# Preparing the second pass's weights later, and taking chunk one last: one core of Trainium2

## The chip, the cores and the metric

The kernel runs on one core of a Trainium2 chip. The metric is the device time of one execution in microseconds (us), as the median of several. The core has TensorE (PE; its weight loads are listed apart as PEld), VectorE (DVE), ScalarE (ACT), GpSimd (POOL), and SyncE (SP), which here issues the DMAs.

## The reference

```python
scores = scale * np.matmul(q, k.transpose(0, 1, 3, 2))        # 8 batches, 8 heads, 576 x 64
...
mask = (rel >= 0) & (rel < window)                            # window 128
scores = np.where(mask, scores + bias[None], -1000000000.0)   # bias: -slope * |i - j|
...
attn_out = np.matmul(attn, v)                                 # softmax of scores, times v
x = attn_out.transpose(0, 2, 1, 3).reshape(B * S, H * D)      # 4608 x 512
h = x @ w_in                                                  # 512 x 2048
sp = np.maximum(h, 0.0) + np.log1p(np.exp(-np.abs(h)))
g = h * erf(sp)
out = g @ w_out                                               # 2048 x 512
```

## The kernel before

**Attention.** It runs in 48 steps, one for the same pair of heads in all that a load `qk` brings; the names carry the step's number: `qk44`, the scores of step 44 on PE (line 635), the masked rows `p44` and sums `st44` on DVE (669), exponentials on ACT (677), scaling on POOL (700), a transpose on DVE (717, `pa44`) and the product with v on PE (739). Four steps make one chunk of 384 tokens of x. There are 12 chunks. All but the first few go through DRAM (`xd`, written at line 791, read as `xr` at 942 or, in the second pass, as `y` at 1113).

**The feed-forward part, first pass** (`one_pass`). Every matrix product is made of three TensorE products of fp32r values: high part by high part, high by low, low by high. The hidden axis of 2048 is cut into 16 tiles of 128 (in the names: `wti`, `wto` 0 to 15 for a tile of w_in or w_out). The first pass takes tiles 0 to 5 of each chunk, 72 units in all, with their weights resident in the tile `w1`; it is interleaved with attention. A unit is a product with w_in (line 977), a copy of its 128x384 sum out of a PSUM bank into `hs` (959 on ACT or 963 on DVE; this pass has one such bank), and later a product with w_out (1053). In between, the activation of several units is made together (a flush, `activate`): softplus and erf on ACT with three table loads (1020, 1022, 1024), a multiplication on DVE (1032), a cast `gh` and a remainder `gl` (1036). After a chunk's six units its output sums go to DRAM as `pd0` to `pd35`, one for 128 tokens (1071).

**Second pass** (`blocks_pass`). The other ten tiles are taken as five pairs, p = 0 to 4, for six double chunks C of 768 tokens: 30 rounds R. A round multiplies a 2x2 block of w_in by a 2x2 block of x in seven products instead of eight (`pair`, products at 1158, their sums combined at 1164 to 1169), activates, and multiplies with w_out (1196: 36 matmuls, three for each of two hidden tiles and six token tiles). Each round fetches its weights from DRAM (`fetch`, 1102: `wi`, 1792 KB, and `wo`, 1024 KB). In a double chunk's last round `store` (1062) loads the first pass's sums (`ot<-pd`, 1073), adds PE's sums on DVE (1074) and stores the result (1079). There are `OB` = 3 buffers `ot`.

**Pair weights.** What `fetch` reads is prepared once by `Weights.pair` (865). For each pair two tiles of w_in and two of w_out are decoded (`decode`, 806: a raw load `wri` or `wro`, one step on ACT or POOL at 823/825, one on ACT at 831, three on DVE at 834, 836, 838), four sums are made for the seven products (876 to 879, `ws`), and each of the parts wa, wb, wc, wd (w_in) and we (twice, w_out) is split into high and low (`split`, 853: a cast at 959 to 963, a subtract at 859) and stored to DRAM (861). The fetch of `wi4` waits for the stores of all four parts of pair 4. The first raw load of each pair waits for the load of one head-pair step, number `WN + p * WD`.

**What sets the order.** Nothing is ordered by hand. `Plan.run` (284) simulates all engines at build time and writes each engine's instructions in the order in which it places them. Each operation has an `at`. Among an engine's ready operations whose buffers are free the smallest `at` goes first:

```python
if o.ready > t + self.WAIT[e] + 1e-9 or (best and (best.at, best.seq) < (o.at, o.seq)):
    continue
if fits(o) and all(t + o.costs[e] <= max(free[x], t) + c for x, c in o.costs.items()):
    best = o
```

So `at` is a priority, not a time; on the chip every engine takes its instructions strictly in the order written, and waits at each for its semaphores. `LEAD` and `TM` make the `at` of the first pass (unit U at LEAD + U * TM, and t1 = LEAD + 72 * TM is the start of the second), `TR` that of its rounds, `W2A` and `W2B` that of the pair weights.

Of the kernel before, what the change touches and what calls it, by code (L numbers as in the profile page):

```python
# [8 lines left out]
F32 = mybir.dt.float32  # L9
# [10 lines left out]
P = 128  # L20
WIN = 128
DM = H * D
# [25 lines left out]
TE, NE = 2.0, 28  # L48
TA = 1.8
LL, LP, LT = 18, 6, 0  # L50
TM = 4.3
LEAD = 70
TR = 15.5
XL, XS = 60, 30
MC, MP, MH = 0.01, 16, -20
W1A, W1B, W1C = 20, 5, 0.4
W2A, W2B, WL = 150, 30.0, 36
WN, WD = 18, 1
POOLQ, POOLH, POOLX, POOLG = 0, 0, 0, 0


# [137 lines left out]
class View(Buf):  # L199
# [10 lines left out]

    def __getitem__(self, at):
        return self.all[at]


class Banks:
# [675 lines left out]
class Moe:  # L891
# [170 lines left out]
    def store(self, u, t, po, at):  # L1062
        nc, op = self.nc, self.plan.op
        T = u["c"] * (self.width // P) + t
        ot = Buf(self.op_, [P, DM], F32, "o", OB, f"ot{T}_{u['U']}")
        part = self.part[T]
        nbytes = P * DM * 4
        if self.first:
            op({"DVE": dve(DM), "Act": act(DM, src=0.06)},
               lambda e: self.copy(e, ot.all, po.all), r=[po], w=[ot], at=at)  # L1070
            op(emit=lambda e: nc.sync.dma_start(part.ap, ot.all), r=[ot], w=[part], at=at, **dma(nbytes))
        else:
            op(emit=lambda e: nc.sync.dma_start(ot.all, part.ap), r=[part], w=[ot], at=at - 10, **dma(nbytes))
            op({"DVE": dve(DM)}, lambda e: nc.vector.tensor_tensor(  # L1074
                ot.all, po.all, ot.all, ALU.add), r=[po, ot], w=[ot], at=at)

            def rows(e):
                for o, r0, n in rows_of(T):
                    nc.sync.dma_start(self.out[r0 : r0 + n, :], ot[o : o + n])  # L1079

            op(emit=rows, r=[ot], at=at, **dma(nbytes, len(rows_of(T))))

    def blocks_pass(self, wi, wo, pool, home, gone, time):

        nc, op = self.nc, self.plan.op
        self.first, self.width = False, 2 * CH
        tags = ["o0", "o1", "o2", "h", "a0", "a1"]
        R = 0
        for C in range(self.nt // (2 * CH)):
            x = self.load_blocks(C, time(R), pool, home, gone)  # L1090
            po = [Buf(self.ps, [P, DM], F32, tag, 1, f"q{C}_{tag}") for tag in tags]
            for p in range(NP):
                own, over = home["wi"] if R % 3 == 2 else (Buf(pool, [P, 14 * SB], F32, "wi", 2, f"wi{R}"), [])
                a = self.fetch(wi[p], own, over * (R == 2), 14 * SB, gone, time(R) - WL)
                own = Buf(pool, [P, 4 * DM], F32, "wo", 3, f"wo{R}")
                b = self.fetch(wo[p], own, [], 4 * DM, gone, time(R) - WL + 0.6 * TR)
                self.pair(C, p, R, x, a, b, po, time(R))
                R += 1
# [3 lines left out]
        op(emit=lambda e: nc.sync.dma_start(w.all, src[0].whole.ap), r=[*src, gone], w=[w, *over], at=at, **dma(P * n * 4))  # L1102
        return w

    def load_blocks(self, C, at, pool, home, gone):

        nc, op = self.nc, self.plan.op
        begun = C == 0
        raw = [Buf(self.xp if t == 0 else pool, [P, NK, CH], F32, "xr", 1, f"y{C}_{t}") for t in range(2)]
        half = lambda b, k: Part(b, slice(None), slice(2 * k, 2 * k + 2))  # L1110
        b = [[half(y, k) for k in range(2)] for y in raw]
        for t in range(2):
            op(emit=lambda e, t=t: nc.sync.dma_start(raw[t].all, self.x_dram[2 * C + t].ap),
               r=[gone, *self.x_parts[2 * C + t]], w=b[t], at=at - XL, **dma(P * NK * CH * 4))
        whole = Buf(pool, [P, 6, CH], F32, "xt", 1, f"xt{C}")
        t1, t2, t4 = (Part(whole, slice(None), slice(2 * k, 2 * k + 2)) for k in range(3))

        def minus(out, a, c):
            op({"DVE": dve(2 * CH)}, lambda e: nc.vector.tensor_tensor(out.all, a.all, c.all, SUB),
               r=[a, c], w=[out], at=at - XS)  # L1120

        minus(t1, b[1][0], b[0][0])
        minus(t2, b[1][1], t1)
        minus(t4, b[0][1], t2)
        minus(b[1][0], b[1][1], b[1][0])
        x = {}
        for n, (name, src) in enumerate([
                ("B11", b[0][0]), ("B21", b[0][1]), ("T2", t2), ("T1", t1), ("T3", b[1][0]), ("B22", b[1][1]), ("T4", t4)]):
            over = []
            if name in home:  # L1130
                hi, lo, over = home[name]
            else:
                hi = Buf(self.xp, [P, 2, CH], F32R, "xh", XB, f"yh{C}_{n}")
                lo = Buf(self.xp, [P, 2, CH], F32R, "xl", XB, f"yl{C}_{n}")
            over = over * begun
            op({"DVE": dve(2 * CH, True), "Act": act(2 * CH), "Pool": pool_cast(2 * CH)},
               lambda e, hi=hi, src=src: self.copy(e, hi.all, src.all), r=[src], w=[hi, *over], at=at - XS + 0.01 * n)
            op({"DVE": dve(2 * CH)}, lambda e, hi=hi, lo=lo, src=src: nc.vector.tensor_tensor(
                   lo.all, src.all, hi.all, SUB), r=[src, hi], w=[lo, *over], at=at - XS + 0.01 * n)
            x[name] = hi, lo  # L1140
        return x

    def pair(self, C, p, R, x, wi, wo, po, at):

        nc, op = self.nc, self.plan.op
        first, last = p == 0, p == NP - 1
        hs = [Buf(self.hp, [P, MW], F32, "m", MB, f"hs{R}_{j}", keep=KH) for j in range(2)]
        h = [[Part(y, slice(None), slice(CH * t, CH * t + CH)) for t in range(2)] for y in hs]

        def product(ps, a, c, begin):  # L1150
            xh, xl = x[c]
            ah, al = LEFT[a]

            def emit(e):
                for k in range(2):
                    w = lambda o: wi[:, o + P * k : o + P * k + P].bitcast(F32R)
                    for n, (o, y) in enumerate(((ah, xh), (ah, xl), (al, xh))):
                        nc.tensor.matmul(  # L1158
                            ps[:, :CH], lhsT=w(o), rhs=y[:, k], start=(begin and k + n == 0), stop=(k + n == 3),
                            skip_group_check=not begin)  # L1160

            op({"PE": 6 * f32r_us(CH) + 0.015}, emit, r=[wi, xh, xl] + [ps] * (not begin), w=[ps], at=at + MH)

        def read(ps, to):
            op({"Act": act(CH, src=0.06), "DVE": dve(CH)}, lambda e: self.copy(e, to.all, ps[:, :CH]),
               r=[ps], w=[to], at=at + MH)

        def add(ps, to):
            op({"DVE": dve(CH)}, lambda e: nc.vector.tensor_tensor(to.all, ps[:, :CH], to.all, ADD),  # L1169
               r=[ps, to], w=[to], at=at + MH)  # L1170

        z, v, u = (Buf(self.ps, [P, 512], F32, "z", 2, f"{k}{R}") for k in "zvu")
        product(z, "A11", "B11", True)
        read(z, h[0][0])
        product(v, "A12", "B21", True)
        add(v, h[0][0])
        product(z, "S2", "T2", False)
        read(z, h[0][1])
        product(u, "S1", "T1", True)
        product(z, "S3", "T3", False)  # L1180
        read(z, h[1][1])
        add(u, h[1][1])
        product(u, "S4", "B22", False)
        add(u, h[0][1])
        product(z, "A22", "T4", False)
        read(z, h[1][0])
        g = self.activate([(MW, hs[j], h[j], at + MC, f"{R}_{j}") for j in range(2)])
        for j in range(2):
            gh, gl = g[j]
            for t in range(2 * CH // P):  # L1190

                def mm(e, j=j, t=t, gh=gh, gl=gl):
                    cs = slice(P * t, P * t + P)
                    w = [wo[:, DM * (2 * j + k) : DM * (2 * j + k + 1)].bitcast(F32R) for k in range(2)]
                    for n, (gg, k) in enumerate(((gh, 0), (gh, 1), (gl, 0))):
                        nc.tensor.matmul(  # L1196
                            po[t].all, lhsT=gg[:, cs], rhs=w[k],
                            start=(first and j + n == 0), stop=(last and j + n == 3),
                        )

                op({"PE": 3 * f32r_us(DM) + 0.015}, mm, r=[gh, gl, wo], w=[po[t]], at=at + MP)
                if last and j:
                    self.store(dict(c=C, U=R), t, po[t], at + MP)


@with_exitstack
def tile_kernel(ctx, tc, qk, vb, w_in, w_out, plain, bias, out, nb=B):
# [63 lines left out]
    wo = [pieces(b, 0, 1024, 2048) for b in drams[1]]  # L1271
    for p in range(NP):
        w1.later = [attention.loaded[min(WN + p * WD, len(attention.loaded) - 1)]]
        w1.pair(p, NF1 + 2 * p, wi[p], wo[p], W2A + p * W2B)
    home, c0 = {}, 0
    for name, n, k in (("wi", 14 * SB, 1), ("T1", 2 * CH, 2), ("T3", 2 * CH, 2), ("B22", 2 * CH, 2), ("T4", 2 * CH, 2)):
        if name == "T3":
# [81 lines left out]
```

## Time and profile before

| | us |
|---|---|
| median of 3 runs | 987.21 (986.49 to 991.13) |
| the profiled execution, device time | 984.83 |
| its span in the trace | 983.0 |
| PE busy | 938.8 (95% of the span) |
| DVE busy | 629.5 (64%) |
| ACT busy | 638.5 (65%) |
| POOL busy | 169.6 (17%) |

The span is the time from the first to the last recorded work; the device time is 1.8 us longer. Times of the trace count from the start of the span. The stages on the time axis: attention with the first pass to about 400 us, the rest of the first pass and the first rounds of the second mixed to about 560, then only rounds of the second pass to the end. PEclk is the granted TensorE clock, 1.00 at 2.4 GHz.

### The profile page before, as it was taken

The page shows a single profiled execution, that of the slowest core. Times are in us where ns is not written, and L with a number is a line of the kernel's source. Part 1 is how long each engine was busy: PE and PEld are TensorE (multiplying, and loading weights), DVE is VectorE, ACT ScalarE, POOL GpSimd, SP SyncE. Part 2 cuts the span into 40 slices and gives each one's busy share as a digit, 9 for nine tenths or more (in the row PEclk, how much of TensorE's full clock was granted, in tenths as well). Part 3 has the DMA queues.
Part 4 walks back from the last instruction along what each step waited for, and adds up shares of the span by engine and source line. Part 5 has one row for each costly group of instructions (what it writes and reads, how often), then busy time and mean ns, then how long its engine had stood idle before and what let it go on. Part 6 is the DMA issues. An engine that isn't in the chain of part 4 may idle for free.

```text
span 983.0 us, 26558 instructions
## 1 busy us (share of the span) xinstructions
PE 938.8 (95%) x11080; PEld 815.2 (83%) x11080; DVE 629.5 (64%) x1468; ACT 638.5 (65%) x1290; POOL 169.6 (17%) x304
## 2 busy tenths in 40 slices
PE   8868999999999999999999999999999999999995
PEld 7656878778877787899988898998988899898984
DVE  6888688888888898444565564564464385373432
ACT  7877777777786688565736746656565666566460
POOL 3544244425445443200000000000000000000000
PEclk9998999999999999999999999999999999999998
DMA  7774667788877776471445658566676756855613
GB/s 242 244 235 148 189 212 232 249 267 283 296 271 259 256 229 228 170 279 58 150 176 210 220 197 328 192 260 224 259 261 220 274 208 225 279 213 177 230 43 97
DMA packets 58760, 216.06 MB, mean 220 GB/s; under 512 B 6928, under 2 KB 16144, under 8 KB 50960
## 3 DMA queue, kind: packets, MB, share of 16 engines
q1 hardware_dynamic: 58640, 214.36, 62.8%
q8 instruction: 87, 1.43, 0.6%
q14 instruction: 33, 0.27, 0.1%
HBM read 171.61 MB, written 42.73 MB: 218 GB/s over the span
## 4 chain that ended last, share of the span: by engine, by line
PE 63%; DMA 2%; DVE 1%; POOL 1%; issue 0%; SPq 0%; ACT 0%; DVEq 0%; POOLq 0%
PE banks L1196 24%; PE banks L1158 21%; PE banks L1053 8%; PE banks L977 7%; PE banks L739 2%; DMA ot<-pd 2%; PE banks L635 1%; DMA out_dram<-ot 1%; POOL p L700 1%; DVE ot L1074 0%; DVE p L669 0%; SPq L1079 0%; DVE pa L717 0%; DVE hs L963 0%; SPq L1102 0%
## 5 line engine op out<-in xcount | busy, mean ns | idle before, releaser
L1196 PE MATMUL banks<-wo,gh 128*128 128x512 f32 x720 | 223.6, 391 | 1.3 <-DVE ot L1074 1.3
L959 ACT COPY hs<-banks 128x384 f32<-128x384 f32 x150 | 71.9, 479 | 199.0 <-PE banks L1158 158.4
L700 POOL TENSOR_SCALAR p<-p,st 128x160 f32<-128x160 f32 (+2 forms) x282 | 158.3, 579 | 226.8 <-DVE st L692 148.4
L977 PE MATMUL banks<-xh,w 128*128 128x384 f32 x576 | 170.3, 351 | 8.8 <-ACT hs L959 6.1
L1196 PEld LDWEIGHTS banks<-wo,gh 128*128 128x128 f32 x720 | 133.1, 188 | 22.6 <-DVE ot L1074 2.4
L1053 PE MATMUL banks<-w,gh 128*128 128x512 f32 x432 | 139.9, 405 | 3.1 <-DVE gh L963 1.7
L1196 PE MATMUL banks<-wo,gl 128*128 128x512 f32 x360 | 141.6, 393 | 0.0
L677 ACT ACTIVATE p<-p,st 128x160 f32<-128x160 f32 (+2 forms) x288 | 120.3, 422 | 25.1 <-DVE st L669 23.7
L977 PEld LDWEIGHTS banks<-xh,w 128*128 128x128 f32 x576 | 108.2, 192 | 19.3 <-ACT hs L959 7.6
L1032 DVE TENSOR_TENSOR hs<-s,hs 128x768 f32<-128x768 f32 (+1 forms) x103 | 89.5, 899 | 30.0 <-ACT s L1022 30.0
L1169 DVE TENSOR_TENSOR hs<-banks,hs 128x384 f32<-128x384 f32 x90 | 50.0, 556 | 85.7 <-PE banks L1158 51.1
L977 PE MATMUL banks<-xl,w 128*128 128x384 f32 x288 | 98.5, 342 | 0.5 <-issue 0.5
L1158 PE MATMUL banks<-w,wi 128*128 128x384 f32 x480 | 94.7, 336 | 0.7 <-DVE hs L963 0.7
L1036 DVE TENSOR_TENSOR gl<-hs,gh 128x768 fp32r<-128x768 f32 (+1 forms) x103 | 91.3, 910 | 5.4 <-ACT gh L959 4.2
L1053 PEld LDWEIGHTS banks<-w,gh 128*128 128x128 f32 x432 | 77.3, 189 | 20.1 <-issue 6.3
L1158 PEld LDWEIGHTS banks<-w,wi 128*128 128x128 f32 x480 | 85.1, 188 | 5.7 <-DVE hs L963 1.0
L1053 PE MATMUL banks<-w,gl 128*128 128x512 f32 x216 | 86.0, 398 | 0.1
L1020 ACT ACTIVATE s<-hs 128x768 f32<-128x768 f32 (+1 forms) x103 | 76.2, 793 | 7.2 <-DVE hs L1169 6.8
L1196 PEld LDWEIGHTS banks<-wo,gl 128*128 128x128 f32 x360 | 67.5, 187 | 14.3
L669 DVE CUSTOM_DVE_ANT_0 p<-banks,tables 128x160 f32<-128x160 f32 (+2 forms) x288 | 75.0, 317 | 4.7 <-PE banks L635 4.3
L1022 ACT ACTIVATE s<-s 128x768 f32<-128x768 f32 (+1 forms) x103 | 76.2, 794 | 0.5
L739 PEld LDWEIGHTS banks<-pa,v 32*64 32x64 f32 x4576 | 60.2, 132 | 19.4 <-DVE st L669 9.3
(114 smaller groups left out, 1419.7 us busy)
## 6 DMA issues: line engine op xcount, KB each, us to landing
wi<-wi SPq DMA_DIRECT2D x20, 1792.0 KB, 7.2
wo<-wo SPq DMA_DIRECT2D x30, 1024.0 KB, 7.0
w<-wi SPq DMA_DIRECT2D x10, 1792.0 KB, 7.4
v<-v_b SPq DMA_DIRECT2D x24, 512.0 KB, 4.9
qk<-qk SPq DMA_DIRECT2D x24, 400.0 KB, 5.2
pd<-ot SPq DMA_DIRECT2D x36, 256.0 KB, 4.0
y<-xd SPq DMA_DIRECT2D x12, 768.0 KB, 4.4
ot<-pd SPq DMA_DIRECT2D x36, 256.0 KB, 6.0
```

The source lines that it names most:

```text
L669: nc.vector.tensor_tensor_reduce(out=dst(j), in0=cut(ps[j].all), in1=cut(table[:, half * j + c0 : half * j + c0 + n]), scale=-0.125, scala ...
L677: nc.scalar.activation(dst(j), dst(j), AF.Exp, bias=low[:, j : j + 1], scale=-1.0, accum_out=total[:, j : j + 1])
L700: (nc.vector if e == "DVE" else nc.gpsimd).tensor_scalar(dst, dst, totals[t][:, j : j + 1], 1.0, op0=ALU.mult, op1=ALU.mult)
L739: nc.tensor.matmul(whole[64 * j : 64 * j + 64, first + a, 32 * t0 : 32 * (t0 + n)], lhsT=y.v[rows, 128 * slot + 64 * j : 128 * slot + 64 * ...
L977: nc.tensor.matmul(ps[:, :W], lhsT=ww[:, cs], rhs=xx[:, k], start=(k2 + k + n == 0), stop=(k2 + k + n == 4),)
L1020: A.activation(s[:, :n], hs[:, :n], AF.Softplus)
L1022: A.activation(s[:, :n], s[:, :n], AF.Erf)
L1032: op({"DVE": dve(n)}, lambda e, s=s, hs=hs, n=n: V.tensor_tensor(hs[:, :n], s[:, :n], hs[:, :n], ALU.mult), r=[s, *own], w=[hs], at=at)
L1036: op({"DVE": dve(n)}, lambda e, gh=gh, gl=gl, hs=hs, n=n: V.tensor_tensor(gl[:, :n], hs[:, :n], gh[:, :n], SUB), r=[hs, gh], w=[gl], at=at)
L1053: nc.tensor.matmul(po.all, lhsT=gg[:, cs], rhs=w.all, start=(u["start"] and n == 0), stop=(u["end"] and n == 2),)
L1158: nc.tensor.matmul(ps[:, :CH], lhsT=w(o), rhs=y[:, k], start=(begin and k + n == 0), stop=(k + n == 3), skip_group_check=not begin)
L1196: nc.tensor.matmul(po[t].all, lhsT=gg[:, cs], rhs=w[k], start=(first and j + n == 0), stop=(last and j + n == 3),)
```

## The change

Three things are edited. First, numbers: `LEAD` and `TM` are lowered, so the first pass's priorities come earlier; the raw loads of all pair weights wait for head-pair step 44 (`WN`, `WD`) instead of 18 to 22; and the pair weights' priority is tied to the round that uses them. Second, the second pass takes double chunks 1 to 5 first and 0 last, and the one-off overlays (`begun`) go by round 0 instead of C = 0. Third, the last round, now that of C = 0, gets four more buffers for the sums `ot`: slices (`Strip`) of one tile `ots` in a pool that is otherwise used for x; and in that round the w_out products go tile by tile instead of hidden tile by hidden tile. The stores of chunk 0's rows are one DMA of 128x512 per token tile; other chunks' are partly cut in two or three. Lines of the changed file are 10 to 12 higher up to the store and some 16 to 21 higher behind it.

```diff
-TM = 4.3
-LEAD = 70
+TM = 4.1
+LEAD = 60
...
-W2A, W2B, WL = 150, 30.0, 36
-WN, WD = 18, 1
+W2A, W2B, WL = 40, 8.0, 36
+WN, WD = 44, 0
...
+class Strip(Part):
...
+    @property
+    def all(self):
+        return self.whole.all.rearrange("p a n -> p (a n)")[:, self.c0 : self.c0 + self.n]
...
-        ot = Buf(self.op_, [P, DM], F32, "o", OB, f"ot{T}_{u['U']}")
+        spare = u.get("spare")
+        if spare and t < len(spare):
+            ot = spare[t]
+        else:
+            ot = Buf(self.op_, [P, DM], F32, "o", OB, f"ot{T}_{u['U']}")
...
-        for C in range(self.nt // (2 * CH)):
-            x = self.load_blocks(C, time(R), pool, home, gone)
+        n = self.nt // (2 * CH)
+        for C in [*range(1, n), 0]:
+            x = self.load_blocks(C, R == 0, time(R), pool, home, gone)
...
+        spare = []
+        if last and not C:
+            own = Buf(self.pool, [P, 6, CH], F32, "xt", 1, "ots")
+            spare = [Strip(own, k * DM, DM) for k in range(4)]
...
-        for j in range(2):
+        tiles = range(2 * CH // P)
+        for j, t in [(j, t) for t in tiles for j in range(2)] if last and not C else [(j, t) for j in range(2) for t in tiles]:
...
-                    self.store(dict(c=C, U=R), t, po[t], at + MP)
+                    self.store(dict(c=C, U=R, spare=spare), t, po[t], at + MP)
...
-        w1.pair(p, NF1 + 2 * p, wi[p], wo[p], W2A + p * W2B)
+        w1.pair(p, NF1 + 2 * p, wi[p], wo[p], t1 + p * TR - W2A)
```

What the order becomes, at three places.

ACT ahead of its first table load (the start of the first flush), before; `wqo` and `wuo` are the two decoding steps on ACT, p10 the exponentials of step 10, hs the sums of a unit:

```order
L823 ACTIVATE wqo2_1210<-wro2_1149 128x512
L831 ACTIVATE wuo2_1212<-wro2_1149 128x512
L959 CAST w1_551<-wto1_1180 128x512
L677 ACTIVATE p10_1227,st10_1228<-p10_1227,st10_1228 128x160 x6
L823 ACTIVATE wqo3_1307<-wro3_1178 128x512
L535 COPY xr2_1171<-banks_134 128x384
L831 ACTIVATE wuo3_1339<-wro3_1178 128x512
L959 COPY hs4_2_1345<-banks_134 128x384
L1020 ACT_TABLE_LOAD
L1020 ACTIVATE s0_1353<-hs0_0_758 128x768
```

and now:

```order
L971 COPY hs2_1_1058<-banks_134 128x384
L689 ACTIVATE p9_1070,st9_1071<-p9_1070,st9_1071 128x160 x2
L843 ACTIVATE wuo1_1164<-wro1_946 128x512
L547 COPY xr2_1179<-banks_134 128x384
L835 ACTIVATE wqo1_1182<-wro1_946 128x512
L971 COPY hs4_2_1212<-banks_134 128x384
L1032 ACT_TABLE_LOAD
L1032 ACTIVATE s0_1219<-hs0_0_758 128x768
```

The decoding of w_out tiles 2 and 3, some casts of `w1` and the exponentials of step 10 now stand behind the flush.

ACT and SP in the last of the pair weights, those of pair 4. Now, on ACT (hs3: sums of round 3; its last copy is that of the round's last product) and then on SP:

```order
L971 COPY hs3_1_8355<-banks_134 128x384
L971 CAST gh2_1_8362<-hs2_1_8220 128x768
L971 COPY hs3_1_8355<-banks_134 128x384
L971 CAST wd4_8387<-wti15_8264 128x256
L1032 ACT_TABLE_LOAD
```

```order
L1119 DMA wo3_8279<-wo3_164 128x2048
L873 DMA wi4_160<-wa4_8257 128x1024
L873 DMA wi4_160<-wb4_8308 128x1024
L873 DMA wi4_160<-wc4_8377 128x1024
L873 DMA wi4_160<-wd4_8387 128x2x256
L1119 DMA wi4_8427<-wi4_160 128x3584
L1119 DMA wi6_8433<-wi1_157 128x3584
```

Before, SP stored the same part in the middle of the attention loads (`v44`, `v45`):

```order
L861 DMA wi4_160<-wb4_6383 128x1024
L861 DMA wi4_160<-wc4_6546 128x1024
L529 DMA v45_6802<-v_b 128x896
L861 DMA wi4_160<-wd4_6799 128x2x256
L791 DMA xd10_78<-xs43_6808 128x384
```

The fetch that stood some 40 SP instructions behind the last store now stands right behind it.

SP at the end, before, where three loads stand behind six stores:

```order
L1079 DMA out_0_dram<-ot31_29_11263 64x512
L1079 DMA out_0_dram<-ot31_29_11263 32x512 x2
L1079 DMA out_0_dram<-ot32_29_11271 32x512 x2
L1079 DMA out_0_dram<-ot32_29_11271 64x512
L1073 DMA ot33_29_11576<-pd33_113 128x512
L1073 DMA ot34_29_11578<-pd34_114 128x512
L1073 DMA ot35_29_11580<-pd35_115 128x512
L1079 DMA out_0_dram<-ot33_29_11576 128x512
L1079 DMA out_0_dram<-ot34_29_11578 64x512 x2
L1079 DMA out_0_dram<-ot35_29_11580 128x512
```

and now, where the four loads into `ots` stand some 20 instructions further ahead:

```order
L1089 DMA ot4_29_11263<-pd4_84 128x512
L1089 DMA ot5_29_11271<-pd5_85 128x512
L1119 DMA wo28_11282<-wo3_164 128x2048
L1119 DMA wo29_11387<-wo4_165 128x2048
L1095 DMA out_0_dram<-ots_10921 128x512 x4
L1095 DMA out_0_dram<-ot4_29_11263 128x512
L1095 DMA out_0_dram<-ot5_29_11271 128x512
```

No load stands behind a store of the last chunk any more.

## Rows read from the trace of the kernel before

**Rows 1.** The page, part 1: busy us (share of the span) and instructions of each engine.

```profile
PE 938.8 (95%) x11080; PEld 815.2 (83%) x11080; DVE 629.5 (64%) x1468; ACT 638.5 (65%) x1290; POOL 169.6 (17%) x304
```

**Rows 2.** Stage table; stretch, length, busy us (instructions) by engine, PEclk, DMA share, GB/s.

```profile
25.00:50.00 25.00, 21.07 (x369) 16.27 (x366) 22.28 (x83) 22.18 (x73) 13.99 (x24) 0.93 0.73 247
50.00:75.00 25.00, 17.59 (x447) 14.65 (x440) 21.23 (x62) 19.49 (x55) 10.69 (x18) 0.88 0.76 236
75.00:100.00 25.00, 20.92 (x484) 17.02 (x484) 21.79 (x62) 17.86 (x53) 9.28 (x15) 0.84 0.42 130
100.00:125.00 25.00, 25.00 (x463) 20.81 (x463) 15.57 (x56) 18.66 (x52) 8.34 (x17) 0.94 0.60 185
200.00:300.00 100.00, 95.94 (x2190) 79.46 (x2175) 85.51 (x256) 77.02 (x206) 44.57 (x77) 1.00 0.79 268
400.00:560.00 160.00, 159.00 (x971) 142.93 (x961) 84.17 (x116) 95.28 (x127) 1.38 (x3) 1.00 0.49 180
```

**Rows 3.** Waits of PE, 25 to 100 us: us in total, times, longest.

```profile
PE banks L977 <- ACT hs L959: 6.1, 3, 3.2
```

**Rows 4.** Waits of PE, 100 to 400 us, the longest named one.

```profile
PE banks L739 <- DVE st L669: 2.7, 5, 1.0
```

**Rows 5.** Timeline of ACT ahead of the first table load: start, length, engine, line, instruction.

```profile
67.91 0.62 ACT L959 CAST w<-wto 128x512 fp32r<-128x512 f32 x1
68.68 0.43 ACT L677 ACTIVATE p<-p,st 128x160 f32<-128x160 f32 x1
...
72.10 0.69 ACT L831 ACTIVATE wuo<-wro 128x512 int32<-128x512 uint32 x1
...
73.17 1.28 ACT L1020 ACT_TABLE_LOAD   x1
```

**Rows 6.** Stage table 125 to 400 us, instructions on tiles wti, wto, wb, wc alone, in turn.

```profile
125.00:400.00 275.00, 34.46 (x66) 1.00 (x2) 1.24 (x2) 1.00 0.75 250
125.00:400.00 275.00, 28.08 (x47) 1.24 (x2) 0.61 (x1) 1.00 0.75 250
125.00:400.00 275.00, 3.51 (x5) 1.22 (x2) 1.86 (x3) 1.00 0.75 250
125.00:400.00 275.00, 4.70 (x8) 1.25 (x2) 1.00 0.75 250
```

**Rows 7.** Tiles wd and wi, copy group of line 959, DMA issues (KB, median us to landing).

```profile
L859 DVE TENSOR_TENSOR wd<-wti,wd x5: 414/425/485, 161.0 to 374.3; 128x256 fp32r<-128x256 f32 x5
L959 ACT CAST wd<-wti x1: 390/390/390, 149.8 to 149.8; 128x256 fp32r<-128x256 f32 x1
...
DMA to landing us min/median/max: 2.9/3.8/5.5
...
DMA to landing us min/median/max: 2.9/7.1/15.0
...
L959 ACT COPY hs<-banks 128x384 f32<-128x384 f32 x150 | 71.9, 479 | 199.0 <-PE banks L1158 158.4 <-PE banks L977 40.5
...
wi<-wi SPq DMA_DIRECT2D x20, 1792.0 KB, 7.2
...
out_dram<-ot SPq DMA_DIRECT2D x14, 256.0 KB, 3.9
```

**Rows 8.** Timeline of all engines around the end.

```profile
971.83 0.39 PE L1196 MATMUL banks<-wo,gl 128*128 128x512 f32 x1
...
972.51 0.39 PE L1196 MATMUL banks<-wo,gl 128*128 128x512 f32 x1
974.24 2.03 SPq L1073 DMA_DIRECT2D ot<-pd  x3
977.19 1.32 DVE L1074 TENSOR_TENSOR ot<-banks,ot 128x512 f32<-128x512 f32 x2 [5.60 <-DMA ot<-pd]
977.90 2.37 SPq L1079 DMA_DIRECT2D out_dram<-ot  x4
979.03 0.69 DVE L1074 TENSOR_TENSOR ot<-banks,ot 128x512 f32<-128x512 f32 x1 [0.52 <-DMA ot<-pd]
```

More of the change, by code (lines that the diff above doesn't have):

```diff
@@ L212, in __getitem__, with __init__ @@
         return self.all[at]
+class Strip(Part):
+    def __init__(self, whole, c0, n):
+        super().__init__(whole)
+        self.c0, self.n = c0, n
+    @property
+    def all(self):
+        return self.whole.all.rearrange("p a n -> p (a n)")[:, self.c0 : self.c0 + self.n]
 class Banks:
@@ L1085, in blocks_pass @@
         nc, op = self.nc, self.plan.op
-        self.first, self.width = False, 2 * CH
+        self.first, self.width, self.pool = False, 2 * CH, pool
         tags = ["o0", "o1", "o2", "h", "a0", "a1"]
         R = 0
-        for C in range(self.nt // (2 * CH)):
-            x = self.load_blocks(C, time(R), pool, home, gone)
+        n = self.nt // (2 * CH)
+        for C in [*range(1, n), 0]:
+            x = self.load_blocks(C, R == 0, time(R), pool, home, gone)
             po = [Buf(self.ps, [P, DM], F32, tag, 1, f"q{C}_{tag}") for tag in tags]
@@ L1103, in fetch, with load_blocks @@
         return w
-    def load_blocks(self, C, at, pool, home, gone):
+    def load_blocks(self, C, begun, at, pool, home, gone):
         nc, op = self.nc, self.plan.op
-        begun = C == 0
         raw = [Buf(self.xp if t == 0 else pool, [P, NK, CH], F32, "xr", 1, f"y{C}_{t}") for t in range(2)]
@@ L1187, in pair @@
         g = self.activate([(MW, hs[j], h[j], at + MC, f"{R}_{j}") for j in range(2)])
-        for j in range(2):
+        tiles = range(2 * CH // P)
+        for j, t in [(j, t) for t in tiles for j in range(2)] if last and not C else [(j, t) for j in range(2) for t in tiles]:
             gh, gl = g[j]
-            for t in range(2 * CH // P):
+            if True:
                 def mm(e, j=j, t=t, gh=gh, gl=gl):
```

## The prediction

> **What bounds the kernel now.** I began with the page: TensorE (PE) is busy for 938.8 us, 95% of the span [rows 1], and no edit of this change alters the number or the shapes of its matmuls. So only the remaining 44 us can be won, plus whatever a lower TensorE clock costs, and every new wait of PE is lost in full. The stage table [rows 2] tells where the 44 us lie. Between 25 and 100 us PE is busy 21.07, 17.59 and 20.92 of each 25 us, 15.4 us short in all, at a granted clock of 0.93, 0.88 and 0.84; 1.00 means the 2.4 GHz level throughout, so PE spent part of these stretches, the ones in which it keeps stopping, at 1.2. Between 200 and 300 us PE is at 95.94 of 100 at full clock, and from 400 to 560 us at 159 of 160. The same rows show the helpers. VectorE (DVE) is busy 21 to 22 of 25 us and ScalarE (ACT) 18 to 22 in the front, DVE 85.51 of 100 in the attention stretch, but only 84.17 of 160 from 400 to 560 us. That hole is where the change puts the weight work. The longest waits of PE from 25 to 100 us [rows 3] are for ACT's copy of a sum out of the single PSUM bank (line 959): 6.1 us in three waits, up to 3.2 each. Last I read the timeline around the end [rows 8]: PE's last matmul begins at 972.51 us and runs 0.39, but the span ends at 983.0, so 10.1 us follow the last product.
>
> **The change part by part.**
>
> *Front.* The pair weights' raw loads wait for a later head pair, and LEAD and TM start the first pass earlier in the scheduler's eyes. In the order of the instructions PE has the same work ahead of its first w_out product (line 1053), but ACT has less ahead of its first table load: six exponentials (0.43 each [rows 5], 2.6 us), four more lowering or unit steps net (0.69 each, 2.8 us) and three casts net (0.62 each, 1.9 us); an x cast and copy against two pa copies about cancel. That is 7.3 us of ACT work, and DVE is relieved of a like amount (softmax rows of one head pair, the decoding of two w_out tiles). ACT is at 22.18 and 19.49 of 25 us there [rows 2] and PE waits for its copies [rows 3], so the first table load, now at 73.17 us [rows 5], should come about 7 us sooner, with the first flush. The postponed work is not gone: it returns after about 80 us, and the cover is the stretch from 100 to 125 us, where PE is busy in full while DVE needs only 15.57 and ACT 18.66 of 25 us [rows 2]. I take **-7 us**. Lower end 2 us: if the two helpers are just as late again afterwards, only part of the 6.1 us of copy waits [rows 3] goes. Upper end 11 us: all PE idleness of 25 to 75 us (3.9 + 7.4 [rows 2]).
>
> *Attention stretch, 125 to 400 us.* The preparation of the five pairs leaves it: instructions on wti tiles kept DVE 34.46 us, those on wto 28.08, wb 3.51 and wc 4.70 [rows 6], 70.8 us together, a quarter of that stretch. PE's named wait there, for DVE's softmax statistics, is only 2.7 us in five waits [rows 4]. Less DVE load may take some of it, the first pass that now runs further ahead may put some back: **-1 us** (0 to -2.7). Where chunk 4's attention output goes through DRAM to become the first pass's input, the order now leaves PE about as much other work as two landings take; I put **+0.5** (0 to 1).
>
> *The transition, about 360 to 520 us.* All 70.8 us of DVE work [rows 6] now start near head pair 44. Between that head pair's scores and the first product that needs the weights of pair 4 (wi4) the order gives PE 351 matmuls of 512 columns, 402 of 384 and some 350 small ones of attention. Three of 512 columns take 0.68 us (the starts at 971.83 and 972.51 [rows 8]), so 80 us, 68 at three quarters of that each, and some 12 for the rest: 160 us. DVE must in that time do some 63 us of preparation (the 70.8 less two wti tiles done before, one wto tile and parts of we left for after), beside its own work: 0.526 (84.17 of 160 [rows 2]) of 160 is 84, together 147; summed instruction by instruction along the order, neighbours overlapping, I get 140. The last link is the part wd4: DVE subtracts, the part is stored to DRAM, and wi4 is fetched whole from there. In the order ACT's cast of wd4 stands behind the copy of round 3's last product. Behind that product PE has only 51 matmuls on wo1 and wo2 left ahead of wi4, 17 times 0.68: 11.6 us. Against that: copy 0.48, cast 0.39, subtract 0.43, store 3.8, fetch 7.2 [rows 7], 12.3 us. The bare chain is 0.7 us late. If DVE is itself the limit it must be through in 160 - 11 = 149 us; at the 0.89 it reached from 25 to 50 us [rows 2] its 140 us take 157 (8 late), its 147 take 165 (16 late). The longest landing of a wi transfer, 15.0 us [rows 7] instead of 7.2, alone would add 8. I take **+5 us**, between the bare chain and the 8 of a DVE at its best share, since the decoding waits for no result of PE and can fill pauses that softmax couldn't; the ends are 0 and 16. The other weights have more room: wi3 about 3 us, the others 10 or more. Those fetches, and the raw loads that SP now issues later, I cost at nothing: the hole from 400 to 560 us has a DMA share of 0.49 [rows 2], and SP waits there in front of work that has room; if it doesn't, what comes late next is wi3.
>
> The Trainium skill, "DMA: Bandwidth & Descriptors", section "Anatomy of one DMA - SWDGE (gpsimd) path", gives a fit of 2.0 us plus the bytes at 436 GB/s; by an estimate from it store and fetch of these sizes would take 2.6 + 6.2 us, 2.2 less than the rows, which would put the bare chain 1.5 us ahead of need and the sum below at about 4 to 5 us less. The rows here were measured under this kernel's own traffic and on another issuing engine, so the sum keeps to them.
>
> *Tail.* Today three loads ot<-pd go out at 974.24, since only three buffers exist and stores of the first three must land first; DVE waits 5.60 us for them, adds from 977.19, adds again at 979.03 (0.69), and 3.3 us later the span ends [rows 8]. In the change the last chunk is chunk 0, six loads stand ahead of the last rounds, and nothing but PE's product is left to wait for. With tiles outermost, five of six tiles are added and stored while PE still works. After the last matmul come one add (0.69), and one store (3.3): 4.1 with the hand-overs instead of 10.1, **-6.0 us** (-5 to -6.5: 256 KB out landed in 3.9 at the median [rows 7]).
>
> *Sum*, on the profiled execution's 984.83: -7 - 1 + 0.5 + 5 - 6 = -8.5, so 976.3. The median of the runs, 987.21, lies 2.4 above the profiled one: **978.7 us**. A difference of 0.5% (4.9 us) is about what can be told from no change here: faster is below 982.3, slower above 992.1.
>
> **The rivals.**
>
> *The front gives nothing.* PE's work there is unchanged, and DVE is at 0.85 of the time until 400 us [rows 2]; if DVE's total and not its order holds PE back in the front, the postponed work catches up with PE after 80 us. For it: DVE 21.79 of 25 from 75 to 100. Against it: the first three waits are ACT's copies, and 100 to 125 us has room. Then 984.83 - 1 + 0.5 + 5 - 6 + 2.4 = 985.7, no change.
>
> *DVE becomes the bound of the transition, and the kernel is slower.* Its place is the in-order DVE queue between head pair 44 and wd4; the price is what DVE needs beyond 149 us. At the attention stretch's share of 0.855 the 147 us take 172, 23 late. It turns the sum positive once wi4 lands more than 13.5 us late, and past the bound of 0.5% from 18.4 late, which is a share under 0.88 with the larger count of work, or 0.84 with the smaller. Time: 984.83 - 7 - 1 + 0.5 + 23 - 6 + 2.4 = 996.7. For it: that share is what DVE reached while PE idled for it. Against it: its pauses there were waits for other engines' softmax steps, of which 63 us of weight work have few.
>
> *The weights come in time.* DVE fills its pauses, the fetch takes less than 7 us and the front gives its upper end: 984.83 - 11 - 1 - 6 + 2.4 = 969.2.
>
> *The tail doesn't do what it says*, if a slice of a pool tile makes all six sums wait for each other: then three stores leave together after the last add, as the four of the last tiles began to do at 977.90 [rows 8]; six stores issued in about the 2.37 us of those four leave the tail a gain of some 4 instead of 6, and the time is 980.7, in the range.
>
> **How the numbers follow.** My forecast with a wait of up to 8 us: 0.54. In time and more: 0.14. No gain in front, or a wait of 9 to 18 us: 0.20. DVE as the bound: 0.12. Faster 0.68, same 0.20, slower 0.12. The range goes from 968 (front 11, attention 2.7, wait and hand-over 0) to 990 (front 2, wait about 11); above it lies the DVE rival, below it next to nothing.
>
> **What would show it.** Right: first table load near 66 us instead of 73.17; copy waits of 25 to 100 us under 4 us; a PE wait at the first wi4 product of some 5 us; no DVE wait for ot<-pd at the end, and 4 us from PE's last matmul to the end of the span. Wrong: PE idle at several places of 360 to 520 us, with DVE above 0.9 there; or a first flush no earlier than 72 us.

## The result, and the profile after

The changed kernel takes 974.29 us (median of 4 runs, 971.19 to 977.34) against 987.85 for the kernel before (4 runs): a ratio of 0.9858, interval 0.9818 to 0.9898. It is faster by 13.6 us; the prediction was 978.7, 8.5 below the 987.21 of before's first three runs. A second measurement, with nothing edited, gave 0.9812 (0.9768 to 0.9857). Times of the kernel before differ from chip to chip by some us, so below each run is told by its ratio to the kernel before on its own chip. The profiled execution of the change took 977.34 us, its span is 975.6.

The stage table of the changed kernel, with the stretches and columns of [rows 2]:

```profile
25.00:50.00 25.00, 19.47 (x334) 14.55 (x334) 21.39 (x74) 21.90 (x70) 14.27 (x24) 0.93 0.73 238
50.00:75.00 25.00, 21.34 (x479) 18.34 (x482) 22.94 (x67) 22.75 (x60) 8.36 (x15) 0.93 0.68 219
75.00:100.00 25.00, 23.53 (x439) 19.54 (x423) 21.85 (x60) 19.15 (x43) 6.99 (x12) 1.00 0.44 136
100.00:125.00 25.00, 22.72 (x403) 18.55 (x402) 17.29 (x55) 18.23 (x47) 10.74 (x18) 0.93 0.47 141
200.00:300.00 100.00, 97.80 (x2119) 81.67 (x2118) 66.60 (x213) 67.21 (x195) 34.78 (x72) 1.00 0.57 175
400.00:560.00 160.00, 155.83 (x1117) 135.88 (x1116) 139.60 (x239) 113.05 (x174) 10.71 (x16) 1.00 0.82 299
```

PE's idleness from 25 to 100 us fell from 15.4 to 10.7 us, and the mean granted clock from 50 to 100 us rose from 0.88 and 0.84 to 0.93 and 1.00. So the front has two gains of about the same size: 4.7 us of stops, and some 5 us of full-speed time that the clock gave back (25 us times 0.05 and 0.16). DVE went from 85.51 to 66.60 of 100 us between 200 and 300 us and from 84.17 to 139.60 of 160 from 400 to 560: most of the 70.8 us of weight work [rows 6] has moved there. PE pays there: 155.83 of 160 busy instead of 159.00.

PE's waits of the changed kernel from 25 to 100 us, then from 420 to 970 us (us in total, times, longest):

```profile
PE banks L751 <- DVE st L681: 3.0, 1, 3.0
PE banks L600 <- POOL p L712: 2.8, 4, 1.2
PE banks L989 <- ACT hs L971: 2.0, 4, 0.6
...
PE banks L1217 <- DVE ot L1090: 2.9, 5, 0.9
PE banks L1065 <- ACT ot L971: 2.2, 1, 2.2
PE banks L1178 <- DVE hs L1189: 1.6, 2, 1.3
PE banks L1178 <- DMA wi<-wi: 0.2, 1, 0.2
```

The copies that cost 6.1 us [rows 3] cost 2.0; the longest wait is now one of 3.0 us for DVE's sums `st`. The expected wait for wi4 (last row) is 0.2 us. The first table load on ACT (row 1) and the end (the others), from the timeline of the changed kernel, as in [rows 5, 8]:

```profile
63.34 1.28 ACT L1032 ACT_TABLE_LOAD   x1
...
971.24 1.69 SPq L1095 DMA_DIRECT2D out_dram<-ot  x2
971.45 0.39 PE L1217 MATMUL banks<-wo,gl 128*128 128x512 f32 x1
971.88 0.69 DVE L1090 TENSOR_TENSOR ot<-banks,ot 128x512 f32<-128x512 f32 x1 [0.67 <-PE banks L1217]
```

The table load comes 9.8 us sooner. DVE's last add waits for PE alone, and from PE's last matmul (971.84) to the end of the span (975.6) there are 3.8 us instead of 10.1.

**An account of PE's time.** To see in which stage a kernel loses time, I took the matmuls that PE began by a given time, by shape, and subtracted what they need at full rate from the time elapsed: 0.2267 us for 512 columns (three in 0.68, [rows 8]), three quarters of it for 384, and small constants, the same for all kernels, for the small matmuls. What is left is time lost to waits, slow clock and uneven pace together. It is worked out from the groups of the trace, one trace for each kernel, in us. One trace is one execution, and the executions of a kernel differ; the last column says by how much the traced one was slower (+) or faster (-) than the median of its kernel on the same chip:

| kernel | 0 to 100 | 100 to 400 | 400 to 560 | 560 to 940 | this execution |
|---|---|---|---|---|---|
| before, first trace | 31.2 | 34.1 | 5.3 | 9.4 | -2.4 |
| before, second trace | 32.9 | 44.2 | 5.7 | 8.4 | +3.8 |
| tail only | 31.5 | 41.8 | 5.7 | 11.2 | +1.6 |
| weights early (LEAD, TM, tail) | 21.4 | 48.1 | 6.4 | 11.6 | +3.0 |
| LEAD, TM as before (late weights, tail) | 31.9 | 23.9 | 12.8 | 11.6 | -6.5 |
| the change | 21.7 | 34.7 | 10.6 | 12.0 | +3.1 |
| the change again | 23.2 | 32.6 | 10.3 | 10.7 | +1.0 |
| no tail (LEAD, TM, late weights) | 22.5 | 30.0 | 12.2 | 9.0 | +0.1 |
| one pair prepared | 21.8 | 26.9 | 5.5 | 10.2 | -2.5 |
| weights at step 36 | 22.3 | 33.2 | 16.0 | 11.7 | +4.4 |
| LEAD 55, TM 4.0 | 24.2 | 24.0 | 15.9 | 11.8 | +0.1 |
| LEAD 55, TM 4.0, weights at 42 | 25.6 | 30.1 | 12.2 | 11.2 | +3.3 |

The spread matters most from 100 to 400 us. The two traces of before and the tail-only one show the same order of instructions up to 560 us, and lose 34.1, 44.2 and 41.8 there. The two traces of the change, the one without its tail and the two of "The end, in two halves" also share one order up to 560 us; they lose 34.7, 32.6, 30.0, 31.7 and 36.3 (the last two worked out in the same way). So a difference of a few us between two single traces says little by itself in this stretch.

### The profile page after: what moved, and what is told of

It is laid out like the page before. It is cut to its first block, busy times and chain, and to the rows that moved or that the text cites. A ratio compares the mean times of both kernels' runs of the same rounds, so it can differ in the third digit from the quotient of the medians.

```text
span 975.6 us, 26523 instructions
## 1 busy us (share of the span) xinstructions
PE 938.7 (96%) x11080; PEld 812.5 (83%) x11080; DVE 640.8 (66%) x1485; ACT 636.0 (65%) x1282; POOL 148.4 (15%) x295
## 4 chain that ended last, share of the span: by engine, by line
PE 69%; DMA 12%; DVE 7%; issue 2%; POOL 2%; ACT 2%; SPq 0%; DVEq 0%; POOLq 0%; ACTq 0%
PE banks L1217 20%; PE banks L1178 16%; PE banks L1065 13%; PE banks L989 12%; PE banks L751 5%; PE banks L647 3%; DMA ot<-pd 3%; DMA out_dram<-ot 3%; DMA xr<-xd 2%; POOL p L712 2%; DMA wi<-wa 1%; DMA y<-xd 1%; DVE p L681 1%; DVE pa L729 1%; DMA wi<-wi 1%
## 5 line engine op out<-in xcount | busy, mean ns | idle before, releaser
L971 ACT COPY hs<-banks 128x384 f32<-128x384 f32 x143 | 68.3, 478 | 173.5 <-PE banks L1178 136.0
L712 POOL TENSOR_SCALAR p<-p,st 128x160 f32<-128x160 f32 (+2 forms) x282 | 141.3, 520 | 262.3 <-DVE st L704 231.4
```

The lines of the kernel that those rows point to most:

```text
L712: (nc.vector if e == "DVE" else nc.gpsimd).tensor_scalar(dst, dst, totals[t][:, j : j + 1], 1.0, op0=ALU.mult, op1=ALU.mult)
```

## The experiments

**The parts one by one.** The edits fall into three: LEAD and TM, the time of the weights, and the tail. In each of these runs one or two are as changed, the rest as before.

*Tail only:*

```diff
-TM, LEAD = 4.1, 60
+TM, LEAD = 4.3, 70
-W2A, W2B = 40, 8.0; WN, WD = 44, 0
+W2A, W2B = 150, 30.0; WN, WD = 18, 1
-        w1.pair(p, ..., t1 + p * TR - W2A)
+        w1.pair(p, ..., W2A + p * W2B)
```

> The change's tail alone (chunk 0 last, four more buffers, tile by tile), with LEAD, TM and the time of the pair weights as before. My theory: the end after PE's last matmul goes from 10.1 us to about 4, and nothing else moves: 6 us faster than before, 981 to 982, ratio 0.994. Rival (what the tail wins is lost by taking chunk 0 last, for instance in the first rounds on chunk 1): under 3 us faster. Rival (the tail is most of the whole gain): 10 us or more.

Measured: 0.9952 (0.9925 to 0.9979), some 4.7 us. The end itself is as expected, 3.7 us from PE's last matmul, a gain of 6.4; but "nothing else moves" doesn't hold: from 560 to 940 us it loses 11.2 where the kernel before loses 9.4 and 8.4.

*No tail:*

```diff
-        for C in [*range(1, n), 0]:
+        for C in range(n):
-            own = Buf(self.pool, [P, 6, CH], F32, "xt", 1, "ots")
-            spare = [Strip(own, k * DM, DM) for k in range(4)]
-        for j, t in [(j, t) for t in tiles for j in range(2)] if last and not C else ...
+        for j, t in [(j, t) for j in range(2) for t in tiles]:
```

> The change without its tail: LEAD, TM and the late weights as changed, chunks in order 0 to 5, three buffers, hidden tile by hidden tile. My theory, by the first trace (PE's last matmul to the end of the span 3.8 us instead of 10.1): 6 us slower than the change, about 980.5, so 7 us faster than before. Rival (the whole gain is the tail's and the rest cancels): within 2 us of before.

Measured: 0.9878 (0.9848 to 0.9908), 12 us faster than before without any of the tail, more than the 7 expected. So the tail is the smaller part of the gain. The stretch from 560 to 940 us shows what taking chunk 0 last costs: 9.0 here, 10.2 to 12.0 in the nine traces of the table that take it last. Most of it is seen as a wait: PE for the adds into ot at the ends of chunks, from 560 to 940 us, in the kernel before, in this kernel and then in the tail-only one:

```profile
PE banks L1196 <- DVE ot L1074: 1.3, 2, 0.9
```

```profile
PE banks L1214 <- DVE ot L1090: 0.9, 2, 0.5
```

```profile
PE banks L1217 <- DVE ot L1090: 2.4, 2, 1.4
```

In the three traces with chunk 0 first this wait is 0.5 to 1.3 us, 0.9 in the mean; in the nine with chunk 0 last it is 2.1 to 3.7, 2.8 in the mean. That is 1.9 of the 2.4 us by which the means of the last stretch differ.

*Weights early*, the tail and LEAD and TM as changed:

```diff
-W2A, W2B = 40, 8.0; WN, WD = 44, 0
+W2A, W2B = 150, 30.0; WN, WD = 18, 1
-        w1.pair(p, ..., t1 + p * TR - W2A)
+        w1.pair(p, ..., W2A + p * W2B)
```

> LEAD, TM and the tail as changed, but the pair weights' raw loads and priority as before (head-pair steps 18 to 22). The first 75 us of ACT's order are the same as in the change. My theory: the front gain of the changed order stays (first table load near 63 us), the transition has no wait, but the attention stretch keeps its DVE load of 0.86: within 3 us of the change, 973 to 978. Rival (late weights are what carries the gain): 979 or more. Rival (late weights cost their wait): 970 or less.

Measured: 0.9922 (0.9894 to 0.9949), 983.1 us. The rival came true: the gain needs the late weights. The front is won as in the change (table load at 62.95 us, 21.4 lost by 100 us), and then mostly lost again: of 10 us there some 3 are left against the tail alone (0.9952). The stage table from 100 to 300 us and the longest wait of PE there, of this kernel, then the stage table of the change:

```profile
100.00:300.00 200.00, 182.64 (x3804) 149.31 (x3803) 164.83 (x473) 145.83 (x391) 81.39 (x133) 0.99 0.75 252
```

```profile
PE banks L989 <- ACT hs L971: 5.6, 2, 3.0
```

```profile
100.00:300.00 200.00, 194.16 (x4221) 161.83 (x4220) 131.10 (x432) 134.21 (x380) 67.19 (x138) 0.99 0.54 166
```

With the weight work in this stretch DVE is busy for 164.83 of 200 us, and PE for 182.64; with it gone 131.10 and 194.16. That the weight work costs PE this time is shown; that DVE's load does it is not, since ACT's load (145.83 to 134.21) and the DMA share (0.75 to 0.54) fall with it, and PE's longest wait with early weights is for ACT's copies. No run takes the load off one of the three alone.

*LEAD and TM as before*, late weights and tail as changed:

```diff
-TM, LEAD = 4.1, 60
+TM, LEAD = 4.3, 70
```

> Late weights and the tail as changed, but LEAD 70 and TM 4.3 as before, so the first table load stands behind the same ACT work as before. My theory: the front gain goes, first table load near 73 us: 981 to 983, 7 to 8 us slower than the change. Rival (the later weights free the attention stretch and the front matters nothing, because the helpers' work is only postponed): within 2 us of the change.

Measured: 0.9925 (0.9895 to 0.9955), a median of 985.3. The front gain is gone as expected (table load at 74.09 us, 31.9 lost by 100 us). The attention stretch of its trace loses least of all, 23.9; but that execution is the fastest of twelve, 6.5 us under their median, and the kernel with LEAD 55 below loses as little, 24.0, with an earlier first pass. What makes it so small is not shown.

Together: tail 0.9952; with LEAD and TM 0.9922; with late weights 0.9925; with both 0.9858 and 0.9812. Each of the two alone adds about 3 us to the tail, both 9 to 14. That is 3.6 to 8 us more than the sum of the two, but with intervals of 3 to 4 us on each ratio the first figure is not clear of the noise and the second just is. The traces give the reason: the earlier first pass wins 9 to 10 us in the front, and with the weight work still in the attention stretch most of it is lost there again. So the two seem to need each other.

**The change again**, as it is:

> The change itself, nothing edited, beside the next runs on one chip. Ratio 0.985 to 0.987 to before, if the first measurement (0.9858) holds; over 0.99 would mean that the gain is smaller than first measured.

Measured: 0.9812 (0.9768 to 0.9857), on the chip of the next three runs. The gain holds; its size is not known better than to some 5 us.

**One pair prepared.** What the weight work still costs where it now lies (this kernel leaves out work that the result needs; it serves the measurement only):

```diff
-    for p in range(NP):
+    for p in range(1):
         w1.later = ...
+    wi, wo = [wi[0]] * NP, [wo[0]] * NP
```

> The change with four of the five weight preparations left out: only pair 0 is prepared and every round fetches its weights, so the decoding, splitting and storing of the other pairs is missing while PE's matmuls, the fetches and the rest stay. My theory now (late weights cost the transition almost nothing, DVE works in its pauses): within 3 us of the change, no more PE busy share won than about 2 us from 400 to 560. Rival (the preparation still costs, only spread over many short waits): 5 us or more faster than the change.

Measured: 0.9711 (0.9669 to 0.9754), 9 us less than the change. The rival is right: late preparation is not hidden. The table above puts 5 of these us between 400 and 560 and 6 to 8 between 100 and 400. Most of the latter is no cost of the preparation: up to about 375 us this kernel has the order of the change, and from 100 to 370 us it lost 24.6 us already, against 26.2 to 31.8 in the five traces with the change's order, by the same account. From 370 to 560 us it loses 7.8, and those five 13.8 to 19.4: that puts the price at 6 to 12 us. The stage table of this kernel from 400 to 560 us, and its two named waits there:

```profile
400.00:560.00 160.00, 159.00 (x1000) 142.38 (x1000) 92.98 (x130) 98.41 (x138) 5.27 (x9) 1.00 0.56 203
```

```profile
PE banks L1178 <- DVE hs L975: 0.7, 1, 0.7
PE banks L1178 <- ACT hs L971: 0.3, 1, 0.3
```

PE is back at 159.00 of 160, with DVE at 92.98 instead of 139.60. In the change PE is idle for 4.2 us here, and 4.0 of it is in four named waits (rows above): one of 2.2 us for ACT's copy of a sum into `ot`, two for DVE's sums `hs`, 1.6 together, and 0.2 for wi4. Which engine's share of the preparation costs what is not separated: with DVE's load, ACT's (113.05 to 98.41) and the DMA share (0.82 to 0.56) go down too.

**Weights at step 36:**

```diff
-WN, WD = 44, 0
+WN, WD = 36, 0
```

> Raw loads of the pair weights wait for head-pair step 36 instead of 44, so the preparation starts some 65 us sooner and has more room ahead of the first rounds. My theory (DVE's load in the attention stretch is what the late start saves): DVE busier from 300 to 400 us, PE idle there up, 0 to 4 us slower than the change. Rival (the late start costs waits in the transition): faster than the change by 2 us or more.

Measured: 0.9829 (0.978 to 0.9877), 2.9 us slower in the median than the change beside it; the intervals overlap, so that is not told apart. DVE is busier from 300 to 400 us, as expected (80.58 of 100 against 71.24), and the time lies within what was expected; but PE's busy time there hardly fell (94.02 of 100 against 95.02 and 94.43), so the reason given for it is not borne out. The transition of this trace loses more, 16.0, though the weights have more room; it is the slowest of the six executions, 4.4 us above their median, and its granted clock there was 0.96 instead of 1.00. The rival, a gain of 2 us or more, is not seen.

**An earlier first pass still:**

```diff
-TM, LEAD = 4.1, 60
+TM, LEAD = 4.0, 55
```

> LEAD 55 and TM 4.0 instead of 60 and 4.1, all else as changed: six instructions fewer on ACT ahead of the first table load. If what stands ahead of the first flush sets the front, the table load comes 2 to 4 us sooner than 63 us; with DVE free in the attention stretch that lead should be kept: 1 to 4 us faster than the change. Rival (attention is bound by the time its helpers need in all): no change or slower, with PE idle moving into 150 to 400 us.

Measured: 0.9802 (0.9758 to 0.9846), the same as the change. The table load comes at 58.31 us and the first product of the second pass at 470.08 instead of 477.51 in the second trace of the change: 7 us won up to there. By 560 us 2 of them are left by the table, and the spans differ by 1.1. Its waits of PE from 420 to 560 us:

```profile
PE banks L1178 <- DMA wi<-wi: 2.1, 1, 2.1
PE banks L989 <- DVE hs L975: 1.6, 2, 0.9
PE banks L1178 <- DVE hs L1189: 1.3, 2, 0.9
PE banks L1178 <- DVE hs L975: 1.2, 2, 1.0
```

Here the wait for late weights is real, 2.1 us, beside three on DVE.

**The same with the weights at step 42:**

```diff
-WN, WD = 44, 0
+WN, WD = 42, 0
```

> LEAD 55 and TM 4.0 as in the run before, and the raw loads of the pair weights at step 42 instead of 44, so that the weights have some 20 us more: there the lead of 7 us that this kernel had at the start of the rounds was lost again from 450 to 560 us, 2.1 us of it at the fetch of wi4. Theory (the weights are late there): 2 to 4 us faster than with 44, ratio 0.977. Rival (DVE's load, not the start, sets it): the same as with 44 or slower.

Measured: 0.9812 (0.9779 to 0.9845): no gain, so the rival stands. In the traces, what the transition won (12.2 lost instead of 15.9) the attention stretch lost (30.1 instead of 24.0); this one is 3.3 us slower than its kernel's median, so part of that is the spread. No complete kernel of this study is faster than the change beyond its interval.

**The end, in two halves** (one execution each). Three buffers, else as changed:

```diff
-            own = Buf(self.pool, [P, 6, CH], F32, "xt", 1, "ots")
-            spare = [Strip(own, k * DM, DM) for k in range(4)]
```

> The change with three buffers for the last sums instead of seven; chunk 0 last and tile by tile stay. My theory (the buffers, not the order of the tiles, take the loads out of the end): loads of the last three sums wait for stores again, though these start 5 us ahead of PE's last matmul: PE's last matmul to the end of the span about 7 us, against 3.8 in the change and 10.1 before. Rival (tile by tile alone does it): under 5.

Its end, from the timeline:

```profile
972.96 0.39 PE L1214 MATMUL banks<-wo,gl 128*128 128x512 f32 x1
973.24 0.69 DVE L1090 TENSOR_TENSOR ot<-banks,ot 128x512 f32<-128x512 f32 x1 [3.24 <-DMA ot<-pd]
...
975.26 0.69 DVE L1090 TENSOR_TENSOR ot<-banks,ot 128x512 f32<-128x512 f32 x1 [0.44 <-DMA ot<-pd]
```

The span ends at 978.9, 5.5 us behind PE's last matmul: the loads wait for stores again, but those start earlier than in the kernel before. That is between the two expectations: chunk 0 last (with its stores in one piece) and tile by tile, not told apart, give 4.6 of the 6.3 us at the end, the further buffers 1.7.

Buffers as changed, products hidden tile by hidden tile:

```diff
-        for j, t in [(j, t) for t in tiles for j in range(2)] if last and not C else ...
+        for j, t in [(j, t) for j in range(2) for t in tiles]:
```

> The change with the last round's w_out products hidden tile by hidden tile again; buffers and chunk order as changed. My theory: six adds follow one another at 0.68 us each with PE's last matmuls and the last stores land close together: 4 to 5 us from PE's last matmul to the end, 0.3 to 1 more than the change. Rival (the order of the tiles matters as much as the buffers): 6 or more.

```profile
972.03 1.37 DVE L1090 TENSOR_TENSOR ot<-banks,ot 128x512 f32<-128x512 f32 x2
972.28 0.39 PE L1217 MATMUL banks<-wo,gl 128*128 128x512 f32 x1
972.75 1.01 SPq L1095 DMA_DIRECT2D out_dram<-ot  x2
```

The span ends at 976.5, 3.8 us behind PE: the same as in the change. With seven buffers the order of the tiles does nothing that one execution shows.

**The kernel before, a second trace:**

> The kernel before, nothing edited, for a second trace of it. Theory (the first trace was a quick execution, its runs spread over 984 to 1000 us, and the spread arises in the attention stretch where DVE is loaded to 0.86): a span of 985 to 990 us, with the time lost beyond the first trace between 100 and 400 us and none behind 560. Rival (the spread arises elsewhere): the loss from 100 to 400 us as in the first trace.

It took 996.29 us, its span 994.5, more than expected. From 560 us on it loses 8.4, and in front 32.9, as the first trace does within 2 us; from 100 to 400 us it loses 44.2, 10 more. The tail-only kernel, whose order is that of before up to 560 us, loses 41.8 there. Of the 10 us, 7 are PE's stops that are put down to issue (15.8 us against 8.8); the waits named after an engine hardly differ (2.9 against 2.7). From 100 to 300 us in the first trace of before, and in the second:

```profile
100.00:300.00 200.00, 191.55 (x4243) 158.02 (x4243) 163.73 (x497) 151.22 (x408) 83.43 (x147) 0.99 0.76 248
```

```profile
100.00:300.00 200.00, 185.46 (x4103) 152.91 (x4100) 156.43 (x475) 143.83 (x388) 77.47 (x135) 0.97 0.74 235
```

Of three traces with this order, the one on which the prediction was worked out lost least in the stretch that the late weights relieve.

## Why the prediction was right, and where not

*Front, -7.* Right in kind, a little small, and with a term that was left at nothing: the sum counted ACT's work and no clock, and the granted clock gave back some 5 us between 50 and 100 us, beside 4.7 us fewer stops. Up to 100 us the changed kernel loses 9.5 (first traces) less, and the table load comes 9.8 us sooner. The run with LEAD and TM as before and the run with early weights show that these two numbers alone do it, not the late weights.

*Cover from 100 to 125 us.* PE was idle for 2.3 us there in the change, where it had been busy in full; but before's second trace has 2.2 idle in the same stretch, so this tells neither for the cover nor against it. That the lead survives the attention stretch is the late weights' doing. The rival "the front gives nothing" is close to what happens with early weights, where most of the lead is lost by 400 us.

*Attention, -1.* This is the step that failed. I priced DVE's relief by the one named wait, 2.7 us in the attention stretch [rows 4]. With LEAD and TM as changed, the traces make late weights worth 13 to 16 us from 100 to 400 us (48.1 against 34.7 and 32.6); with them as before, 10 to 20 (23.9 against 34.1, 44.2 and 41.8). Both are likely too large, since the trace with early weights is a slow execution and that with 23.9 the fastest of twelve. The ratios give 6 to 11 us with LEAD and TM as changed (0.9922 to 0.9858 and 0.9812) and 3 with them as before (0.9952 to 0.9925), after the cost in the transition; with the 4 and 7 us more that the transition loses, the stretch itself gains some 10 to 15. That is still far from 1. The one named wait was not the measure: stops put down to issue hold most of what before's slower traces lose more than its first (7 of 10 us), and with early weights PE waits 6.7 us for ACT's copies, a wait that the trace of before does not name in this stretch. Against the first trace of before, the change's own trace shows nothing of the gain (34.7 against 34.1), since that was a quick execution; the runs' medians do.

*Transition, +5.* The size was right, the place was not, so the size is luck. From 400 to 560 us the change loses 5 more than before (10.6 and 10.3 against 5.3 and 5.7), and the run with one pair shows that the preparation is the cause. But PE's wait for wi4, which was to be the price, is 0.2 us. In the trace of the change the store of wd4 was issued at 542.33 us, the fetch 2.3 us later, on landing, and PE was ready for wi4 at 552.3:

```profile
542.33 0.38 SPq L873 DMA_DIRECT2D wi<-wd  x1
544.67 0.80 SPq L1119 DMA_DIRECT2D wi<-wi  x2
...
552.53 0.41 PE L1178 MATMUL banks<-yh,wi 128*128 128x384 f32 x1 [0.20 <-DMA wi<-wi]
```

The store landed after 2.2 us instead of the median 3.8 [rows 7], which alone makes 0.9 early of 0.7 late; the fetch landed 7.7 us after its issue instead of 7.2, and the hand-overs between the steps took the rest. By the fit of the Trainium skill, "DMA: Bandwidth & Descriptors", section "Anatomy of one DMA - SWDGE (gpsimd) path", made for transfers that GpSimd issues, an estimate for the two is 2.6 and 6.2 us. For this store it is nearer than the median was, for this fetch it is 1.5 us short. DVE was busy for 139.60 of 160 us, a share of 0.87, and for 46.14 of 50 from 450 to 500, a share of 0.92, above the 0.89 that I had taken for its best. So DVE worked at a higher share than the 0.855 on which the rival "DVE as the bound, and slower" rested, and that rival's price did not come. DVE was not the only one that PE waited for either: of 4.0 us of named waits 2.2 are for ACT.

*Tail, -6.* The end gained 6.3, as forecast, and the rival of slices that wait for each other is out: the adds start one after another at 965.08, 966.44, 967.80 us. What I missed, and put at nothing, is that taking chunk 0 last costs 2 to 3 us in the rounds before, so that tail only gives 4.7. The longer waits for the adds into `ot` hold about 1.9 of it; why the adds come later there was not found.

*Hand-over, +0.5.* No wait of the changed kernel at that place is named; too small to tell.

*The sum.* On the two traces it comes out near the forecast, span 983.0 to 975.6, 7.4 against 8.5, but in part by luck: the front's 2.5 us more and the 2.6 us lost from 560 to 940 us, which had no term, cancel. The medians moved by more, 13.6 and 18.6: the attention stretch varies in before's order, and two of the three traces of it lost 8 to 10 us more there than the one that I read. Of the rivals, "in time and more" (969.2) lies nearest in its first half: the weights came in time.

## What to carry to other kernels

The waits that are put down to a busy engine by name are no upper bound for what moving its work away is worth: 2.7 us were named, some 10 to 15 won. What the stretch loses in all (time elapsed less the time that its matmuls need, 34 to 44 us here) is one, though a wide one. Two edits can need each other: starting PE's work earlier paid little here while the weight work lay in the stretch that follows, so each alone was a poor measure of both. And a single trace may be a lucky one: where the runs of a kernel spread over several us, look at two traces before the sum is made.

## What the runs showed of the hardware

The same order of instructions lost 34.1, 41.8 and 44.2 us from 100 to 400 us in three traces; the granted clock of 100 to 300 us was 0.99, 0.98 and 0.97 in them, and PE busy 191.55, 186.38 and 185.46 of 200. From 560 to 940 us, where PE hardly stops, the two traces of before differ by 1.0. What sets the difference off was not found.
